# Moving two casts, four groups of transposes and one weight load by one step in a fused attention and SwiGLU kernel

## The chip, the cores and the metric

The kernel runs on one NeuronCore of one Trainium2 chip. The metric is the device time of one execution in microseconds; lower is better. The engines are named as the profile names them: PE is TensorE, PEld its weight loads, DVE is VectorE, ACT is ScalarE, POOL is GpSimd, SP is SyncE, which here only issues DMAs.

## The reference

Attention with a causal mask and a bias of cumulated sums, then a feed-forward block on the result (numpy, shortened):

```python
# q, k, v: (8, 8, 576, 64); s: (8, 8, 576); 4608 tokens, d_model 512, d_ff 1536
scores = scale * q @ k.T
cum = cumsum(maximum(s, 0))
scores = where(causal, -1e9, scores + minimum(-(cum[:, None] - cum[None, :]), 0))
attn = softmax(scores)
x = (attn @ v).transpose(0, 2, 1, 3).reshape(4608, 512)
out = (silu(x @ w_gate) * (x @ w_val)) @ w_out
```

Inputs and output are float32.

## The kernel before

All matrix products run in bfloat16. The work is one long list of instructions for each engine, written out in program order: each engine executes its own list from the top, and semaphores make it wait for the others. So the place of a call in the Python code sets the place of its instructions on every engine's list.

**Attention.** There are 64 heads, numbered 0 to 63 over batches (8 heads each). Four heads are a half batch (`hb`): half batch 2 is heads 8 to 11, half batch 3 is heads 12 to 15. For each half batch k and q are loaded as float32 (`load_one`, line 140, tiles `rawk` and `rawq`), cast to bfloat16 (`cast_one`, line 246 where GpSimd does it, tiles `ck` and `cq`), transposed and copied into the operand tile `kq`. For half batches 0 to 4 the transposition is done by TensorE: `pe_transpose` (line 287) makes five or four 128x128 transposes into a PSUM bank, and `pe_out` copies the two halves of the bank to `kq` (line 314 on ScalarE, line 316 on VectorE). `prep_one(hb, i)` is one such group: i = 0 and 2 are the two groups of k, 1 and 3 those of q. It issues the transposes and the first copy; the second copy goes on the list `seconds`, from which one is taken after every feed-forward item.

A head's scores are made in four pieces (`score_piece`, matmuls line 359, Exp on ScalarE line 369, tile `pt`). From head 8 on the causal mask is put on by a select on GpSimd after pieces 0 and 3 (lines 374 and 379). The attention-times-v products (`av_piece`, line 396) follow some heads later, and are normalised by VectorE (lines 412 and 413). v is cast in five chunks (`cast_v`, line 168, tile `vt`) as listed in `V1_AT`.

**Feed-forward.** 4608 tokens are taken in nine tiles of 512 (`tt`). Each tile has 12 gate blocks and 12 value blocks (`block`, line 629, four 128x512 matmuls each), a Tanh on ScalarE (line 650), two products on VectorE (lines 652 and 663), and then the down projection (line 686 for the first two tiles, line 735 for the others). Gate and value blocks are named here by their number: gate 5 is the sixth gate block of a tile.

**What sets the order.** The last loop of the kernel weaves the two together. `ffn_items(tt)` yields after every block or part of the down projection; its sum of costs is `n`. After each item the functions listed for this number by `at_item` are called, and then `pump` runs as many attention steps as belong to the share of the tile that is done. Inside `attn_items`, after piece `ci` of the head at place `step` of half batch `h`, the table `PREP_AT[h]` may call `prep_one` for the next half batch; for h = 2 ScalarE makes the copies if `ci` is 0 or 1, VectorE if it is 2 or 3. PSUM has eight banks; `take` gives the one that was released longest ago, in program order.

The stretch that the change touches lies in tile 0 of the feed-forward: heads 9 to 11 (half batch 2) are scored beside gate and value blocks 4 to 8, while k and q of half batch 3 are cast and transposed. Their loads were issued from GpSimd's list earlier. The output weights are loaded in two halves by `w_load("o", j)` (line 332), also issued by GpSimd. The v chunks of batch 1 and k and q of half batches 4 and 5 are issued by SP.

Of the kernel before, what the change touches and what calls it, by code (L numbers as in the profile page):

```python
# [19 lines left out]
def kernel(  # L20
# [11 lines left out]
    nc = tc.nc  # L32
# [77 lines left out]
    with tc.manual_schedule():  # L110
# [415 lines left out]
        def prep_one(hb, i, eng=None):  # L526
# [6 lines left out]
            seconds.append(lambda: pe_out(hb, nm, g, 1, eng))  # L533

        PREP_AT = {
            2: {(1, 2): 0, (2, 0): 2, (2, 2): 1, (3, 0): 3},
            3: {(1, 3): 0, (2, 1): 1, (2, 3): 2, (3, 1): 3},
        }

# [455 lines left out]
        def at_item(n, f, *args):  # L995
            hook[n].append(lambda: f(*args))

        at_item(2, prep_one, 2, 2)
        at_item(8, cast_one, 3, "k", nc.gpsimd)
        at_item(9, cast_one, 3, "q", nc.gpsimd)  # L1000
        at_item(10, w_load, "o", 0)
        at_item(12, w_load, "o", 1)
        for tt in range(NTT):
            lo = H * (tt + 1) + LAGS[tt]
# [60 lines left out]
```

## Time and profile before

| | us |
|---|---|
| median of 3 runs | 376.75 (376.2 to 377.3) |
| profiled execution: its own time | 375.79 |
| profiled execution: span of its instructions | 374.0 |
| TensorE busy | 360.7 |
| VectorE busy | 289.6 |
| ScalarE busy | 240.4 |
| GpSimd busy | 212.3 |
| DMA bandwidth, mean over the span | 172 GB/s |

The span is the time from the first to the last instruction; the device time of the same execution is 1.8 us longer. A matmul starts before the one in front of it has ended, so the busy time of TensorE holds no overlap twice, and distances are best counted from start to start. In a timeline, rows in a row with the same line are merged (x4), and a bracket gives the idle time of the engine before the row and what ended it. Some records of matmuls are missing, so that a block can be shown with three instead of four.

### The profile page before, as it was taken

Reading aid. Unit: us, or ns where it says so; the run is one execution under the profiler, and the core shown is the slowest. Engines: PE = TensorE matmul, PEld = TensorE weight load, DVE = VectorE, ACT = ScalarE, POOL = GpSimd, SP = SyncE. Lnnn points to the kernel's source line nnn. Section 1 sums busy time; section 2 is a strip of 40 time slices with the busy share of each in tenths; the row PEclk is TensorE's granted clock in tenths of the full one; section 3 lists DMA queues with packets and bytes.
Section 4 is the critical chain, followed back from the end, with each engine's and each line's share of the span. In section 5 each row is a group of like instructions: output and inputs, shape, how many; then the busy total and the mean of one; then the engine's idle time right before and its main releaser. Section 6 shows DMA issues by size and latency. Waiting matters only on the chain.

```text
span 374.0 us, 8759 instructions
## 1 busy us (share of the span) xinstructions
PE 360.7 (96%) x3259; PEld 230.6 (62%) x3300; DVE 289.6 (77%) x578; ACT 240.4 (64%) x471; POOL 212.3 (57%) x325
## 2 busy tenths in 40 slices
PE   7799899999999999999999999999999999999995
PEld 6584456655555556855685559655865585476464
DVE  8968776468995899588967997699858867975984
ACT  8777677698876877588757875686566523323321
POOL 8883555856455647494649464955675516315320
PEclk9999999999999999999999999999999999999999
DMA  7899999799877997896779675984132103002003
GB/s 239 193 258 253 219 257 267 237 303 247 245 186 220 254 262 196 178 281 205 211 167 266 178 182 174 255 206 98 40 119 62 35 19 128 2 0 95 20 0 114
DMA packets 97146, 64.23 MB, mean 172 GB/s; under 512 B 77232, under 2 KB 82736, under 8 KB 97104
## 3 DMA queue, kind: packets, MB, share of 16 engines
q1 hardware_dynamic: 84976, 41.46, 45.2%
q0 software_dynamic: 12128, 22.21, 22.6%
q8 instruction: 26, 0.43, 0.5%
q14 instruction: 16, 0.13, 0.1%
HBM read 37.90 MB, written 19.86 MB: 154 GB/s over the span
## 4 chain that ended last, share of the span: by engine, by line
PE 85%; DMA 6%; POOL 5%; ACT 1%; issue 1%; DVE 1%; DVEq 0%; POOLq 0%; ACTq 0%
PE bank L629 45%; PE bank L735 17%; PE bank L359 10%; PE bank L396 7%; PE bank L686 5%; DMA rawk<-in_k_dram 4%; DMA rawv<-in_v_dram 2%; POOL rawv L157 1%; POOL vt L168 1%; POOL wv L332 1%; ACT pt L369 1%; PE bank L287 0%; POOL rawq L140 0%; ACT kq L314 0%; POOL kq L211 0%
## 5 line engine op out<-in xcount | busy, mean ns | idle before, releaser
L369 ACT ACTIVATE pt<-bank 128x512 bf16<-128x512 f32 (+1 forms) x256 | 120.4, 510 | 31.0 <-PE bank L359 18.2
L629 PE MATMUL bank<-XT,wg 128*128 128x512 bf16 x418 | 110.3, 379 | 1.2 <-DVE pp L652 0.3
L629 PE MATMUL bank<-XT,wv 128*128 128x512 bf16 x412 | 109.3, 379 | 1.1
L650 ACT ACTIVATE th<-bank 128x512 bf16<-128x512 f32 x108 | 64.7, 599 | 55.9 <-PE bank L629 53.6
L652 DVE SCALAR_TENSOR_TENSOR pp<-th,bank 128x512 bf16<-128x512 bf16 x108 | 73.6, 682 | 19.2 <-ACT th L650 18.7
L663 DVE SCALAR_TENSOR_TENSOR ht<-pp,bank 128x512 bf16<-128x512 bf16 x108 | 74.1, 686 | 10.6 <-PE bank L629 0.4
L359 PE MATMUL bank<-kq 128*128 128x128 bf16 (+4 forms) x576 | 75.6, 240 | 1.5 <-DMA kq<-HL 1.0
L672 POOL TENSOR_TENSOR ht<-ht 128x512 bf16<-128x512 bf16 x35 | 40.4, 1154 | 52.2 <-DVE su L670 52.1
L359 PEld LDWEIGHTS <-kq 128*128 128x128 bf16 x576 | 45.8, 98 | 31.5 <-issue 1.9
L629 PEld LDWEIGHTS <-wv 128*128 128x128 bf16 x432 | 38.4, 98 | 36.5 <-issue 0.6
L629 PEld LDWEIGHTS <-wg 128*128 128x128 bf16 x432 | 38.3, 98 | 34.2 <-issue 0.7
L396 PEld LDWEIGHTS <-pt 128*128 128x128 bf16 x960 | 41.9, 98 | 17.2
L374 POOL TENSOR_SCALAR_AFFINE_SELECT pt<-pt 128x512 bf16<-128x512 bf16 x56 | 36.8, 658 | 27.3 <-ACT pt L369 22.7
L396 PE MATMUL bank<-vt,pt 128*128 128x65 bf16 x960 | 47.0, 194 | 0.4 <-POOL vt L168 0.3
L430 POOL DMA_DIRECT2D xs<-ot x24 | 21.7, 905 | 30.0 <-DVE ot L413 27.6
L735 PEld LDWEIGHTS <-ht 128*128 128x128 bf16 x336 | 31.2, 98 | 4.3
L413 DVE TENSOR_TENSOR ot<-bank,rc 128x320 bf16<-128x320 f32 x64 | 31.5, 492 | 2.2
L183 POOL DMA_DIRECT2D kq<-HL x48 | 28.9, 604 | 0.0
L735 PEld LDWEIGHTS <-su 128*128 128x128 bf16 x252 | 23.5, 98 | 3.3
L686 PE MATMUL bank<-wo,ht 128*128 128x512 bf16 x90 | 24.8, 379 | 0.3
L800 POOL TENSOR_TENSOR ysb<-ysb 128x512 f32<-128x512 f32 x12 | 15.2, 1270 | 15.3 <-DVE ysb L794 15.3
L379 POOL TENSOR_SCALAR_AFFINE_SELECT pt<-pt 128x64 bf16<-128x64 bf16 x56 | 14.8, 264 | 15.8 <-ACT pt L369 15.7
(93 smaller groups left out, 384.6 us busy)
## 6 DMA issues: line engine op xcount, KB each, us to landing
out_dram<-ysb POOLq DMA_DIRECT2D x32, 256.0 KB, 4.5
rawv<-in_v_dram SPq DMA_DIRECT2D x28, 256.0 KB
rawk<-in_k_dram SPq DMA_DIRECT2D x12, 576.0 KB
rawq<-in_q_dram SPq DMA_DIRECT2D x12, 576.0 KB
xs<-ot POOLq DMA_DIRECT2D x24, 160.0 KB, 3.5
ks<-ck SPq DMA_DIRECT2D x11, 288.0 KB
qs<-cq SPq DMA_DIRECT2D x11, 288.0 KB
rawk<-in_k_dram POOLq DMA_DIRECT2D x3, 576.0 KB, 7.3
```

The lines of the kernel that those rows point to most:

```text
L359: nc.tensor.matmul(sc[:, o : o + w], T[:, 1, e * S + 128 * tj : e * S + 128 * (tj + 1)], T[:, 0, e * S + lo : e * S + hi], start=not maske ...
L369: nc.scalar.activation(pt[:, c0 : c0 + n], sc, AF.Exp, scale=0.125)
L374: nc.gpsimd.affine_select(pt[:, 1088:1600], pt[:, 1088:1600], pattern=[[0, 4], [1, 128]], compare_op=ALU.is_ge, fill=zreg, base=0, channel ...
L396: nc.tensor.matmul(av[:, bi * (D + 1) : (bi + 1) * (D + 1)], pt[:, c0 : c0 + 128], VT[b % 2][:, tj, h, :], start=(tj == 0), stop=(tj == bi),)
L413: nc.vector.tensor_mul(ot[:, :, e * D : (e + 1) * D], av3[:, :, 0:D], rc[:, :, None].to_broadcast([128, NCH, D]),)
L629: nc.tensor.matmul(view(bs, TT), w[:, c, f0 : f0 + 128], xt[:, c, :], start=(c == 0), stop=(c == 3),)
L650: nc.scalar.activation(th, pg, AF.Tanh, scale=0.5)
L652: nc.vector.scalar_tensor_tensor(pp, in0=th, scalar=1.0, in1=pg, op0=ALU.add, op1=ALU.mult)
L663: nc.vector.scalar_tensor_tensor(hp[:, 2 * k2 : 2 * k2 + 2, :].rearrange("p a n -> p (a n)"), in0=pp, scalar=0.5, in1=pv, op0=ALU.mult, op ...
L672: (nc.vector if ft == NFT - 1 else nc.gpsimd).tensor_sub(hp[:, 1:3, :], hp[:, 1:4:2, :], hp[:, 0:3:2, :])
L686: nc.tensor.matmul(view(pys[ts_], DM), hps[ft // 2][:, 2 * (ft % 2) + half, c0 : c0 + 128], WO[j][:, ft % WKO, :], start=(ft == 0), stop=( ...
L735: nc.tensor.matmul(ps, lhs(p), rhs(p), start=(first and p == 0), stop=(last and p == NP - 1), skip_group_check=True,)
```

## The change

Three things move; no instruction is added or removed.

```diff
         PREP_AT = {
-            2: {(1, 2): 0, (2, 0): 2, (2, 2): 1, (3, 0): 3},
+            2: {(1, 3): 0, (2, 1): 2, (2, 3): 1, (3, 1): 3},
             3: {(1, 3): 0, (2, 1): 1, (2, 3): 2, (3, 1): 3},
         }
...
-        at_item(8, cast_one, 3, "k", nc.gpsimd)
-        at_item(9, cast_one, 3, "q", nc.gpsimd)
-        at_item(10, w_load, "o", 0)
+        at_item(9, cast_one, 3, "k", nc.gpsimd)
+        at_item(10, cast_one, 3, "q", nc.gpsimd)
+        at_item(9, w_load, "o", 0)
         at_item(12, w_load, "o", 1)
```

The four groups of transposes for half batch 3 come one score piece later: the first behind piece 3 of head 9 instead of piece 2, the second behind piece 1 of head 10 instead of piece 0, the third behind piece 3 of head 10 instead of piece 2, the last behind piece 1 of head 11 instead of piece 0. The engine of each copy stays the same. The two casts are listed after items 9 and 10 instead of 8 and 9, and the first half of the output weights after item 9, behind the cast of k, instead of after item 10.

## The prediction

> **What bounds the kernel now.** I read the page first: how full is TensorE, and where is it not full.
>
> ```profile
> span 374.0 us, 8759 instructions
> PE 360.7 (96%) x3259; PEld 230.6 (62%) x3300; DVE 289.6 (77%) x578; ACT 240.4 (64%) x471; POOL 212.3 (57%) x325
> ...
> PE   7799899999999999999999999999999999999995
> ...
> PEclk9999999999999999999999999999999999999999
> ```
>
> TensorE is busy 96% of the span at full granted clock, and all slices but the first two and the last are at 8 or 9 tenths. So a change outside TensorE counts only if it removes or adds TensorE idle time. The change works between 38 and 50 us; the waits of 22 to 60 us (total, times, longest) show what TensorE waits for there:
>
> ```profile
> PE bank L287 <- POOL ck L246: 1.2, 1, 1.2
> ...
> PE bank L396 <- POOL vt L168: 0.3, 1, 0.3
> ```
>
> The chain of waits of the same stretch (start, duration, what) says what stands behind these:
>
> ```profile
> 22.81 15.78 DMA rawk<-in_k_dram
> ...
> 38.72 1.15 POOL ck L246
> ...
> 39.92 0.45 PE bank L287 x5
> ...
> 47.45 0.69 DVE pp L652
> ...
> 48.17 0.84 DVE kq L316
> ...
> 49.03 0.70 DVE ht L663
> ...
> 50.55 0.24 POOL pt L379
> ...
> 53.66 0.19 PE bank L396
> ```
>
> Three places follow: the load of k for half batch 3 lands, GpSimd casts it, and the first transposes (39.92) start the moment the cast is done; VectorE's product for value block 7 (49.03) frees the bank of gate block 9 (49.77); a select on GpSimd (50.55) lets the casts of v start, and TensorE waits for the fourth (53.66). Last the timelines of TensorE, of GpSimd and of ScalarE:
>
> ```profile
> 38.38 0.38 PE L359 MATMUL bank<-kq 128*128 128x320 bf16 x2
> 39.92 0.45 PE L287 MATMUL bank<-ident,ck 128*128 128x128 bf16 x5 [1.16 <-POOL ck L246]
> 40.21 0.19 PE L359 MATMUL bank<-kq 128*128 128x64 bf16 x1
> 40.24 1.03 PE L629 MATMUL bank<-XT,wg 128*128 128x512 bf16 x4
> 41.10 0.39 PE L359 MATMUL bank<-kq 128*128 128x128 bf16 x4
> ```
>
> ```profile
> 38.72 1.14 POOL L246 CAST ck<-rawk 128x1152 bf16<-128x1152 f32 x1 [1.51 <-DMA rawk<-in_k_dram]
> ...
> 40.21 1.15 POOL L246 CAST cq<-rawq 128x1152 bf16<-128x1152 f32 x1 [0.35 <-DMA rawq<-in_q_dram]
> 41.30 0.85 POOL L332 DMA_DIRECT2D wo<-in_moe_w_out_dram  x1
> ```
>
> ```profile
> 47.29 0.72 ACT L314 COPY kq<-bank 64x512 bf16<-64x512 bf16 x1
> ...
> 49.02 0.72 ACT L314 COPY kq<-bank 64x512 bf16<-64x512 bf16 x1
> 49.77 1.20 ACT L369 ACTIVATE pt<-bank 128x512 bf16<-128x512 f32 x3
> ```
>
> Matmuls overlap, so I count from start to start. A 128x512 costs 0.216 us, a block of four 0.86 to 0.87 (40.24 to 41.10), a piece 3 of a head 0.03, a piece 2 0.22. The first transposes were due at 38.38 + 0.22 = 38.60 and began at 39.92: **1.32 us lost**. Gate 9 was due at 49.47 (piece 0 of head 12 at 49.25 plus 0.22) and began at 49.77: **0.30 lost**. The tenth product of head 8's first attention-times-v piece was due at 53.22 and began at 53.66: **0.44 lost**. After it TensorE's largest idle time is 0.12 us, at 85.49; small gaps of 0.05 are rows where a matmul record is missing.
>
> **The change, part by part.** It adds and removes no instruction. Comparing the built orders:
>
> *Casts.* On GpSimd only the cast of q and the first output-weight issue change places; the cast of k stays where it was. So its time stays too: it waits for a landing that TensorE does not influence, and ends at 39.86.
>
> *First transposes.* Between piece 2 of head 9 and these transposes TensorE now has piece 3 (0.03) and gate 5 (0.86). They are due at 38.60 + 0.89 = 39.49 and still start at 39.92: 0.43 lost instead of 1.32, **0.89 saved**. Both items that move forward wait for banks released by 37 us.
>
> *The rest of the stretch, to gate 9.* The other three transpose groups and their eight copies to kq also move one piece later. On ScalarE the Tanh of gate 6 started at 43.31 and that of gate 7 at 46.81; between them stand two kq copies, two 512-wide Exps, then a 64-wide and a 512-wide Exp. The changed order has the same six there. VectorE then has product, kq copy, product (47.45, 48.17, 49.03 to 49.73) in both orders. Gate 6 ends 0.89 earlier, so the chain does, and gate 9 starts at 48.88; TensorE's own due time moves as much (48.58), so the 0.30 stays lost. Nothing gained or lost here.
>
> *A new tight place.* The last transposes now follow head 11's piece 1 and gate 8: 46.83 - 0.89 + 0.21 + 0.87 = 47.02, done at 47.41. Their first copy on ScalarE comes behind gate 8's Tanh (47.2 to 47.7), so about 47.70 to 48.40. Head 12's piece 0, the first reader, is due at 48.36: 0.1 late where it was 1.2 early. That 0.1 hides in the wait before gate 9; gate 8, value 8 and the pieces of head 11 are the cover. If the copy is over 0.3 late, every further tenth is lost.
>
> *v casts.* The second copy of the last q group (49.02) stood in front of head 11's pieces 2 and 3 on ScalarE; now it stands behind them. Piece 2 starts at 48.44 after the first copy. Its row at 49.77 was followed by the select at 50.55 (+0.78) and the fourth v cast's end at 53.60 (+3.05). The same steps give 49.22 and 52.27. TensorE wants it at 53.22 - 0.89 = 52.33: the 0.44 goes, **0.4 saved**. If ScalarE is as late as before relative to TensorE, none of it goes. The v loads that these casts read had landed by 50.97 by their semaphore events; the cast of the last one comes at about 52.2.
>
> *Output weights.* Issue (0.85) from 39.86 instead of 41.30; the cast of q then runs 40.71 to 41.86, 0.5 later. Its reader, the third transposes, stands at 43.7: 1.9 us of cover. Queued behind on GpSimd are the selects of heads 9 and 10 and the second weight issue, none read before 50 us. At no cover this would cost 0.5. The weights are read from 57 us on; the first landed at 51.69.
>
> *DMA.* 1.4 us earlier the weight load can take packets from SP's queue, which carries v (batch 1) and k, q of half batch 4. The landed load of k was at hand when its cast started at 54.30 without a wait; its transposes, at 57.58 before, would be due at 56.25. With the cast's 1.14 the load may land until 55.1. Even if all 1.4 us were taken from it, from the 53.87 of its semaphore events, the delay costs 0.2. I take nothing: the software queue was still full with older weights until 45.47 (wv's landing). By the Trainium skill ("DMA: Bandwidth & Descriptors", section "Queues, rings and completion order") each DMA engine takes turns between queues packet by packet, which speaks against issuing weights early: by it SP's loads would give up about half of 1.4 us, an estimate of 0.7, and the sum would still not change, as 53.87 + 0.7 is within the limit.
>
> *To the end.* From head 12's first attention-times-v piece on, the orders of all engines agree but for bank names, so whatever TensorE is ahead at 53 us, it stays ahead, unless a transfer is late. Nearest: half batch 6's transposed k landed at 93.32, and the copy reading it on VectorE began at 93.77. Ahead by 1.3, that copy waits up to 0.9. At 127.35 the same copy waited 0.34 and TensorE lost nothing.
>
> **Sum.** 0.89 + 0.44 = 1.33. On the profiled execution's own time, 375.79 (span 374.0, 1.8 around it, unchanged): 374.46. That execution lies 0.96 under the median, 376.75; on the median 375.4. Bounds: 0.89 alone gives 375.9; with the tight place 0.3 worse, 376.2; with the 0.30 before gate 9 gone too, 375.1.
>
> **Rivals.** *The wait returns at head 12 or downstream.* The first 0.89 is real, but the copies of q are now the last thing ready, or later loads land at fixed times and eat the lead. For: 0.1 late by my own walk, and 1.3 us less room; the 0.45 at 93 us. Against: the copies have only ScalarE's order to fear, and VectorE's wait at 127 us did not reach TensorE. Price: 0.5 to 1.3 given back, 375.9 to 376.75.
>
> *Slower: the early weights push back SP's loads.* Place: the load of k 4, or the last of v, which GpSimd casts in order ahead of everything else. It decides from a landing of k 4 later than 55.1; to end 1.13 over the median it must take back 1.33 + 1.13, so land at 57.6, 3.7 us later than now. For: DMA is saturated there (page: 9 tenths). Against: the issue moves by 1.4 us, no bytes are added. Time 377.9.
>
> *It does nothing:* the cast of k does not move on GpSimd, so were the transposes' wait set by a later landing than the profile's, by 0.4 or more, the saving remains 0.89. Only an earlier landing takes it away: by 0.9 it leaves 0.4 of the 0.89, by 1.3 nothing: 376.3 to 376.75.
>
> **Chances.** Forecast 0.74; given back 0.10; nothing 0.05; slower 0.11. About 0.3%, 1.13 us, is what a measurement of this kernel can tell from no change, so faster begins under 375.6. The forecast's own range, 374.9 to 375.9, lies mostly below that: I put 0.66 of its 0.74 there, and 0.08 inside. Faster 0.66; within 0.08 + 0.10 + 0.05 = 0.23; slower 0.11. Range: 374.5 (the bound 375.1 less 0.6, as the lowest run of before lies 0.55 under its median) to 376.7, which takes in nearly all of the give-back.
>
> **What would show it.** After: transposes of k at 39.9 with an idle of about 0.3 instead of 1.16; gate 5 at 38.63; gate 9 at 48.9; the wait of the attention-times-v product on v under 0.1; the cast of q at 40.7. Wrong: a TensorE wait on the kq copy before head 12's piece 0 over 0.3; gate 9 later than 49.2; a wait of the k 4 transposes at 56; a span above 373.3.

## The result, and the profile after

The changed kernel is slower: 378.95 us (median of 14 runs, 377.27 to 380.65) against 376.16 us (14 runs, 374.42 to 378.36) of the kernel before. The ratio is 1.0074, with a 95% interval of 1.0053 to 1.0096. The forecast was 375.4 us with a range from 374.5 to 376.7. The profiled execution of the changed kernel took 377.27 us, the lowest of its 14. The top of its page:

```profile
span 375.6 us, 8799 instructions
...
PE 363.3 (97%) x3300; PEld 231.1 (62%) x3300; DVE 290.1 (77%) x578; ACT 240.8 (64%) x471; POOL 213.1 (57%) x325
...
PE   7799979999999999999999999999999999999995
...
PEclk9999999999999999999999999999999999999999
```

The averages say almost nothing. (More matmuls are listed than before because fewer records are missing, not because there are more.) The waits from 22 to 62 us (total, times, longest) say where the time went:

```profile
PE bank L396 <- POOL vt L168: 2.5, 1, 2.5
...
POOL vt L168 <- DMA rawv<-in_v_dram: 2.4, 1, 2.4
```

The wait of the transposes (L287) is gone; about 0.3 of it was forecast to stay. But the attention-times-v product's wait on the cast of v, which was to go from 0.44 (counted from start to start; 0.28 by its bracket) to under 0.1, grew to 2.5. The cast itself now waits 2.4 for its load. The chain of waits (start, duration, what) shows the load:

```profile
33.45 21.05 DMA rawv<-in_v_dram
54.51 0.05 issue
54.56 0.63 POOL vt L168
55.19 0.04 issue
55.23 0.19 PE bank L396
55.42 0.86 PE bank L629 x4
```

In the kernel before, what ended this chain at the same place was a select on GpSimd, and the load did not appear. Now chunk 3 of v (batch 1) lands at 54.5; by its semaphore events it landed at 46.75 before. The timeline of GpSimd around it:

```profile
49.75 1.17 POOL L168 CAST vt<-rawv 128x512 bf16<-128x512 f32 x2
50.93 0.64 POOL L374 TENSOR_SCALAR_AFFINE_SELECT pt<-pt 128x512 bf16<-128x512 bf16 x1
51.51 0.61 POOL L168 CAST vt<-rawv 128x512 bf16<-128x512 f32 x1
54.56 1.28 POOL L168 CAST vt<-rawv 128x512 bf16<-128x512 f32 x2 [2.43 <-DMA rawv<-in_v_dram]
```

Chunks 0 to 2 are cast in time, then GpSimd stands still until chunk 3 is there. TensorE at the places that the prediction had put times on, with gate 7 (44.66) between them:

```profile
39.02 0.41 PE L359 MATMUL bank<-kq 128*128 128x320 bf16 x3
39.27 1.03 PE L629 MATMUL bank<-XT,wg 128*128 128x512 bf16 x4
40.13 0.44 PE L287 MATMUL bank<-ident,ck 128*128 128x128 bf16 x5
...
44.19 0.39 PE L359 MATMUL bank<-kq 128*128 128x128 bf16 x4
44.66 1.02 PE L629 MATMUL bank<-XT,wg 128*128 128x512 bf16 x4
...
47.94 1.03 PE L629 MATMUL bank<-XT,wv 128*128 128x512 bf16 x4
48.97 0.38 PE L359 MATMUL bank<-kq 128*128 128x128 bf16 x4
49.19 1.03 PE L629 MATMUL bank<-XT,wg 128*128 128x512 bf16 x4
...
52.25 0.44 PE L396 MATMUL bank<-vt,pt 128*128 128x65 bf16 x9
55.23 0.19 PE L396 MATMUL bank<-vt,pt 128*128 128x65 bf16 x1 [2.54 <-POOL vt L168]
```

To compare these with the trace of before, one offset must be taken off: the first feed-forward matmul (L629) began at 25.80 before and at 26.44 here. That is 0.64 later and lies in front of everything that the change touches. Counted from there, gate 5 stands at 38.63 and gate 9 at 48.55, and the first transposes (40.13) have no idle time at all. Up to 52 us TensorE was ahead as forecast, and somewhat more. Then nine products of head 8 run and the tenth waits 2.54 us.

Why would chunk 3 come late, if no byte was added? The DMA queues in two stretches of 3 us (packets, MB, share of 16 engines): q1 is SP's queue with v, k and q, q0 the software queue, which GpSimd fills, with the weights. The share adds up the times of all packets, which overlap, so it can pass 100%. First the kernel before, 41 to 44 us (upper two lines) and 44 to 47 us (lower two):

```profile
q0 software_dynamic: 442, 0.33, 70.1%
q1 hardware_dynamic: 1202, 0.30, 56.2%
...
q0 software_dynamic: 441, 0.44, 89.6%
q1 hardware_dynamic: 895, 0.22, 34.5%
```

The same stretches of the changed kernel:

```profile
q1 hardware_dynamic: 1785, 0.45, 72.5%
q0 software_dynamic: 320, 0.26, 54.0%
...
q0 software_dynamic: 560, 0.57, 113.1%
q1 hardware_dynamic: 168, 0.04, 10.8%
```

A chunk of v is 1024 packets of 256 bytes. Between the older weights and the output weights the software queue runs empty, engine by engine, and SP's queue then goes fast. By the DMA packets of the trace, in before it carries about 190 packets per us up to 42 us, 347 in the next, then 664 and 723 in the two us from 43 to 45, while q0 falls from about 190 to 158, 93 and 74. I call this the hole. Chunks 2 and 3 go through in it. In the changed kernel the hole is over at 44, and for three us, beside output weights in packets of about 1 KB, SP's queue carries 54 to 58 packets per us. In the changed kernel the output weights were issued at 38.89 (41.30 before) and ended the hole early: of chunk 3, ten of the 16 DMA engines were through by 44.2, and the other six finished at 46.9, 50.0, 51.4, 51.7, 52.1 and 54.5. Over 41 to 47 us SP's queue carried only 144 packets fewer (1953 against 2097), but the load is complete only with its last packet.

### The profile page after: what moved, and what is told of

Read it like the earlier page. It is cut to its first block, busy times and chain, and to the rows that moved or that the text cites. A ratio compares the mean times of both kernels' runs of the same rounds, so it can differ in the third digit from the quotient of the medians.

```text
span 375.6 us, 8799 instructions
## 1 busy us (share of the span) xinstructions
PE 363.3 (97%) x3300; PEld 231.1 (62%) x3300; DVE 290.1 (77%) x578; ACT 240.8 (64%) x471; POOL 213.1 (57%) x325
## 4 chain that ended last, share of the span: by engine, by line
PE 86%; DMA 7%; SPq 2%; POOL 2%; ACT 1%; issue 0%; DVEq 0%; POOLq 0%; DVE 0%
PE bank L629 45%; PE bank L735 17%; PE bank L359 11%; PE bank L396 7%; DMA rawv<-in_v_dram 6%; PE bank L686 6%; SPq L157 2%; ACT pt L369 1%; DMA kq<-HL 1%; PE bank L353 1%; PE bank L287 0%; PE bank L445 0%; POOL kq L214 0%; POOL kq L211 0%; POOL rawk L140 0%
## 5 line engine op out<-in xcount | busy, mean ns | idle before, releaser
L629 PE MATMUL bank<-XT,wg 128*128 128x512 bf16 x432 | 111.4, 379 | 0.4 <-DVE pp L652 0.3
L629 PE MATMUL bank<-XT,wv 128*128 128x512 bf16 x432 | 110.9, 379 | 0.1
L672 POOL TENSOR_TENSOR ht<-ht 128x512 bf16<-128x512 bf16 x35 | 40.5, 1156 | 52.1 <-DVE su L670 52.0
L629 PEld LDWEIGHTS <-wv 128*128 128x128 bf16 x432 | 38.4, 98 | 38.7 <-issue 2.9
L629 PEld LDWEIGHTS <-wg 128*128 128x128 bf16 x432 | 38.4, 98 | 34.2 <-issue 0.7
L686 PE MATMUL bank<-wo,ht 128*128 128x512 bf16 x96 | 25.7, 379 | 0.0
```

Of the source, the lines that this page charges most:

```text
L629: nc.tensor.matmul(view(bs, TT), w[:, c, f0 : f0 + 128], xt[:, c, :], start=(c == 0), stop=(c == 3),)
L672: (nc.vector if ft == NFT - 1 else nc.gpsimd).tensor_sub(hp[:, 1:3, :], hp[:, 1:4:2, :], hp[:, 0:3:2, :])
L686: nc.tensor.matmul(view(pys[ts_], DM), hps[ft // 2][:, 2 * (ft % 2) + half, c0 : c0 + 128], WO[j][:, ft % WKO, :], start=(ft == 0), stop=( ...
```

## The experiments

Theory: the early output weights alone cause the loss, by catching the last packets of chunk 3; the moved transposes are a gain of about 1.3 that this hides. Rivals: the transposes' new place costs something that the walk missed; the weights cost by their bytes and not by where they overtake; the clock after the wait is the larger part. All ratios are to the kernel before on the same chip.

**The weights alone, and the transposes alone.** Two kernels split the change. The first is the kernel before with only the first output weights issued early:

```diff
         at_item(8, cast_one, 3, "k", nc.gpsimd)
+        at_item(8, w_load, "o", 0)
         at_item(9, cast_one, 3, "q", nc.gpsimd)
-        at_item(10, w_load, "o", 0)
```

> The kernel before with one part of the change alone: the first half of the output weights is issued on GpSimd between the casts of k and q of half batch 3; casts and transposes stay. Theory A (the early weights reach the DMA engines before SP's load of v chunk 3 is through them; chunk 3 lands at 54.5 us instead of 46.8, its cast and TensorE wait for it): chunk 3 lands after 50 us, TensorE waits 1 to 2.5 us before the tenth attention-times-v product of head 8, and because that wait ends at a landing, not at TensorE's own pace, the time is the changed kernel's, 378 to 379.5, 0.4% to 0.9% over before. Theory B (the later transposes and kq copies, or the new order of banks, cost the time): no difference from before, within 0.3%, and the first transposes still wait for the cast.

Measured: 379.15 us (6 runs), ratio 1.0079 [1.0053, 1.0105], as slow as the whole change. Its waits from 22 to 62 us:

```profile
PE bank L396 <- POOL vt L168: 3.1, 1, 3.1
...
POOL vt L168 <- DMA rawv<-in_v_dram: 2.7, 1, 2.7
```

Chunk 3 landed at 55.5, with nine of its engines through by 45.2. The first transposes, at their place in the kernel before, waited only 0.08 us here, because k had landed at 38.34 and TensorE came to them 0.8 later. That this is as slow as the whole change is itself a reading: the gain from the transposes cannot show in a kernel where TensorE later waits for a landing, since being early only makes that wait longer.

The second is the changed kernel with the weights issued behind the cast of q again:

```diff
         at_item(10, cast_one, 3, "q", nc.gpsimd)
-        at_item(9, w_load, "o", 0)
+        at_item(11, w_load, "o", 0)
```

> The changed kernel with the weight issue put back behind the cast of q (one 64-wide select later than in the kernel before). Theory A: v chunk 3 lands before 48 us, the wait before the tenth product is under 0.1 us, and the predicted 0.9 to 1.3 us are gained: 374.8 to 375.5, 0.2% to 0.4% under before. Theory B: as slow as the changed kernel, about 379.

Measured: 374.87 us (12 runs), ratio 0.9974 [0.9951, 0.9998]. By the ratio that is 0.98 us less than before, with an interval of 0.1 to 1.8 that holds the predicted 1.33. Its timeline of GpSimd:

```profile
49.79 1.17 POOL L168 CAST vt<-rawv 128x512 bf16<-128x512 f32 x2
50.97 0.63 POOL L374 TENSOR_SCALAR_AFFINE_SELECT pt<-pt 128x512 bf16<-128x512 bf16 x1
51.55 1.72 POOL L168 CAST vt<-rawv 128x512 bf16<-128x512 f32 x3
```

The casts of chunks 2 to 4 follow one another with no bracket: chunk 3 had landed at 47.8. The weights, issued at 41.39, landed at 51.99, as in the kernel before (41.30 and 51.69). This version is faster than both kernels, against the kernel before by an interval that ends just under 1.

**Later still.** The first weights at item 12, the second half at item 15.

```diff
-        at_item(9, w_load, "o", 0)
-        at_item(12, w_load, "o", 1)
+        at_item(12, w_load, "o", 0)
+        at_item(15, w_load, "o", 1)
```

> The changed kernel with both halves of the output weights issued later: the first behind the select of head 10's piece 0 (about 43 us, where the second stood), the second two selects later (about 47 us). Theory A: the software queue stays empty longer after the older weights, v chunk 3 lands by 46 us or earlier and chunk 4 by 50; time as with the weights behind the cast of q or up to 0.3 us better, 374.5 to 375.4, unless the second half, read from about 66 us, comes too late. Theory B: about 379.

Measured: 375.01 us (12 runs), ratio 0.9979 [0.9952, 1.0006]. Chunk 3 landed at 46.2. In its profile the first weights were issued at 41.41, hardly later than in e2 (41.39), not at about 43 as expected; the second half came at 46.00 instead of 42.83. So a later second half won nothing that these runs can tell apart, and a much later first half was not tried. Three of its 12 runs took 377.7 to 380.2 at a mean granted clock of 0.991 to 0.995; what slowed those was not looked into.

**The change again**, with no edit, on another occasion:

> The changed kernel once more, in the same job as the three others, for a second profile. Theory A: v chunk 3 lands after 50 us again, though not at the same time, and the wait before the tenth product is 2 us or more; time 0.5% to 1.0% over before. If the wait is far longer than 2.5 us in this profile, the granted clock should be lower after it, as the recorded runs with clocks of 0.994 and spans of 377.3 against 0.999 and 375.6 suggest.

Measured: 379.91 us (6 runs), ratio 1.0112 [1.0085, 1.0138]; chunk 3 at 55.1. The waits, and then two windows (length, busy time of TensorE, weight load, VectorE, ScalarE, GpSimd, then granted clock, DMA share, GB/s):

```profile
PE bank L396 <- POOL vt L168: 3.4, 1, 3.4
POOL vt L168 <- DMA rawv<-in_v_dram: 3.2, 1, 3.2
```

```profile
54.00:58.00 4.00, 2.20 (x14) 1.09 (x14) 0.24 (x1) 0.00 (x0) 2.14 (x4) 0.61 1.00 361
58.00:62.00 4.00, 4.00 (x28) 2.25 (x27) 1.96 (x6) 1.54 (x3) 2.21 (x3) 0.53 0.77 207
```

Here is a second cost that the first profile did not have: from 54.91 on, the last 0.9 us of the wait and what follows, TensorE's granted clock is 0.5 for 6.8 us, and in 58 to 62 us it gets 28 matmuls done where the first profile of the changed kernel had 57. By the Trainium skill ("TensorE: Matmul & The Clock Gate", section "Part 1: The HAM clock gate (the "warmup" mystery)") the clock falls to half after an idle window of about 3.4 us, and the windows run free of the kernel. The stretches seen here, 3.4 and 6.8 us, are one and two such windows. But the clock also fell after waits of 3.07 and 3.26 us, shorter than the page's window, and did not after 2.54. Where they differ, the runs decide.

The records of the granted clock in the traces show what decides here besides the length: how the wait lies against the windows. All but the last of each trace, which the end cuts off, last whole multiples of 3.41 us, so the windows of each trace can be counted. In the first profile of the changed kernel a new window began at 53.88, in the middle of the wait: 1.19 us of idle time fell into one window and 1.35 into the next, and the clock stayed. In e1, e4, e5 and e7 a single window held 2.78, 2.48, 1.95 and 2.49 us of idle time, and the clock fell at that window's end (55.90, 54.91, 57.04 and 56.18). In e4 it stayed at half for one more window, which held the last 0.89. This is read from five traces; the place of a wait was not varied by itself.

**Bytes or overtaking?** The early weights stay, but chunks 3 and 4 of v go into the same queue, issued by GpSimd ahead of them:

```diff
-        load_v(1, range(5))
+        load_v(1, range(3))
+        load_v(1, (3, 4), nc.gpsimd)
```

> The changed kernel, early weights and late transposes, with chunks 3 and 4 of v (batch 1) issued from GpSimd at about 30 us, in the same software queue ahead of the output weights, instead of from SP. Theory A (the weights overtake these chunks because they come through the other queue): both chunks land before 48 us, no wait before the tenth product, first weights land about 1.5 us later than in the changed kernel; time as with the weights behind the cast of q, 374.5 to 375.5. A rival within A (what counts is the bytes that the early weights add before 50 us, whatever the queue): something else lands late instead, chunk 2 or k of half batch 4, and the time stays above 377.

Measured: 374.63 us (12 runs), ratio 0.9981 [0.9956, 1.0007]. The weights were issued at 39.16, about as early as in the changed kernel, and the same bytes were moved. GpSimd again:

```profile
50.03 1.17 POOL L168 CAST vt<-rawv 128x512 bf16<-128x512 f32 x2
51.21 0.63 POOL L374 TENSOR_SCALAR_AFFINE_SELECT pt<-pt 128x512 bf16<-128x512 bf16 x1
51.79 1.72 POOL L168 CAST vt<-rawv 128x512 bf16<-128x512 f32 x3
```

No wait. Chunks 3 and 4 landed at 46.4 and 47.0. So an early issue by itself costs nothing that these runs can tell apart, nor do its bytes: it costs when it overtakes, from another queue, a load that is needed sooner. The two chunks changed their time of issue with their queue (30.7 and 31.6 instead of 33.5 and 39.2), and the two were not tried apart.

**Earlier still.** The first weights at item 7, issued at 34.65:

```diff
-        at_item(9, w_load, "o", 0)
+        at_item(7, w_load, "o", 0)
```

> The changed kernel with the first output weights issued still earlier, at about 35.5 us, in front of the selects of heads 8 and 9 and of the cast of k. Theory A: the software queue does not run empty at all between the older weights and these, so SP's queue never gets its stretch of 340 to 720 packets per us; chunk 3 and now chunk 2 too land later than in the changed kernel on more engines, chunk 3 at 54 to 57; wait of 3 us or more, half clock after it, 380 to 383. If what counts were only the swap with the cast of q: as the changed kernel, 379.

Measured: 379.47 us (4 runs), ratio 1.0092 [1.0059, 1.0126]. The queues, 41 to 44 us (upper two) and 44 to 47 us (lower two):

```profile
q0 software_dynamic: 525, 0.44, 90.4%
q1 hardware_dynamic: 530, 0.13, 33.7%
...
q0 software_dynamic: 471, 0.47, 92.4%
q1 hardware_dynamic: 464, 0.12, 29.7%
```

The hole is gone: 994 packets of SP's queue in 6 us where before had 2097. Chunk 3 now lands late on all 16 engines (52.2 to 54.5) instead of on six. In the end that costs the same, because only the last engine counts; TensorE waited 3.26.

**Half the size.** Three of the six slices of the first output weights are issued early, the other three at item 15, and the second load (`"o", 1`) at item 16:

```diff
+            if kind == "o" and h is not None:
+                dst, src_ap = dst[:, 3 * h : 3 * h + 3], src_ap[:, 3 * h : 3 * h + 3]
...
-        at_item(9, w_load, "o", 0)
-        at_item(12, w_load, "o", 1)
+        at_item(9, w_load, "o", 0, 0)
+        at_item(15, w_load, "o", 0, 1)
+        at_item(16, w_load, "o", 1)
```

> The changed kernel with only half of the early load (three of six slices of the first output weights) issued at the early place; the other half and the second weights are issued at about 47 us. Theory A: the engines that the early half catches before v chunk 3 is through are free again about 3 us sooner; chunk 3 lands at 48 to 51, its cast comes at its place in GpSimd's order or up to 0.5 us after; time 374.5 to 376. If the early start alone decided, whatever the size: chunk 3 at 54 or later and 379.

Measured: 374.65 us (10 runs), ratio 0.9976 [0.9954, 0.9998]. Issued at 38.66, chunk 3 at 48.2, no wait. It moves the rest of the weights too, so it does not isolate size from what follows: from 47 to 50 us the software queue carried nothing. Together with the late chunk of e7 it fits SP's packets being slowed for as long as any weights, of either half, are queued beside them.

**The clock.** Is the rest of the loss the half clock? Spare 128x128 matmuls on a bank of their own fill the wait for chunk 3, first 36, then 66. They stand in front of the seventh product:

```diff
+                        if p == H:
+                            fill = take()
+                            for _ in range(36):
+                                nc.tensor.matmul(view(fill, 128), ident, ident, start=True, stop=True)
+                            give(fill)
```

> The changed kernel with 36 matmuls of 128x128 on a spare bank (identity by identity, result unused, 36 x 0.056 = 2.0 us) put on TensorE in front of the product that waits for v chunk 3. The wait itself is not shortened. If the idle time alone is the cost (theory A without the clock): 379 to 380, no better than the changed kernel. If, as the two profiles with waits of 3.07 and 3.37 us and a clock of 0.5 for 3.4 and 6.8 us after them suggest, a part of the cost is the granted clock (theory A with the clock): the clock stays at full after the wait, the idle rest is 0.5 to 1.5 us, and 1.5 to 3 us come back: 376 to 377.5. Theory B (transposes or bank order): 379 or more.

Measured: 379.33 us (6 runs), ratio 1.0092 [1.0061, 1.0123]. In its profile 1.95 us of wait were left, chunk 3 came at 55.1, and the clock still fell, to 0.5 for 3.4 us, from 57.04 on, 1.2 us after the wait had ended. In the five other runs the mean clock was 1.0, and yet they took 378.2 to 380.5.

> The changed kernel with 66 instead of 36 spare matmuls in front of the product that waits for v chunk 3 (66 x 0.056 = 3.7 us), so that TensorE is busy through nearly the whole wait, which still ends with the landing at 54.5 to 55.5 us. If the granted clock is a part of the cost: idle rest under 0.5 us, no stretch at 0.5 near 55 us, and about 1.7 us (half of 3.4 us) come back against the changed kernel: 377 to 377.8. If the clock is no part of it, or falls for another reason: 379 to 380, as with 36 spare matmuls, where the idle rest was 1.95 us and the clock fell all the same.

Measured: 378.73 us (9 runs), ratio 1.0095 [1.0063, 1.0128]. The windows of this kernel:

```profile
54.00:58.00 4.00, 3.95 (x71) 3.52 (x70) 0.49 (x2) 0.00 (x0) 1.42 (x3) 1.00 1.04 363
58.00:62.00 4.00, 3.95 (x48) 2.57 (x46) 3.38 (x8) 2.91 (x6) 3.33 (x5) 1.00 0.85 234
```

The clock stays at 1.00 through both. But the time did not come back. In this profile the fill itself ran until 56.59, some 0.8 beyond the end of the cast, which uses up half of what the clock would give. Counted from the first feed-forward matmul, the tenth product came at 30.20 (e5) and 29.77 (e9), later than in the first profile of the changed kernel (28.79), whatever the clock did. So the larger fill keeps the clock up, but these two runs do not show by their times what the half clock costs. That is left to the traces, below.

**The kernel before once more**, with no edit, for a second trace:

> The kernel before, for a second profile of it. The wait of the first transposes for the cast of k was 1.16 us in the first profile, and 0.08 us in the kernel with the early weights alone, whose TensorE order is the same: there TensorE reached the place 0.8 us later and the load landed 0.3 us earlier. If the wait depends on this, it lies anywhere between 0 and 1.2 us here and follows from the landing of k (36.9 to 38.6 in the profiles so far) less TensorE's own arrival; chunk 3 of v lands before 48 us. If it is fixed by the order, it is 1.0 to 1.2 again.

Measured: 376.36 us (one run, span 374.6). Its waits:

```profile
PE bank L287 <- POOL ck L246: 1.2, 1, 1.2
...
PE bank L396 <- POOL vt L168: 0.3, 1, 0.3
```

The load of k landed at 39.16, chunk 3 at 47.2. Both waits that the prediction worked with were there again, 1.24 and 0.28. They are no accident of one execution, though the first was 0.08 in e1.

## Why the prediction was wrong

**Steps that held.** *First transposes* and *the rest of the stretch*: less the offset of 0.64, gate 5 stands at 38.63, the forecast place, and gate 9 at 48.55 (forecast 48.9). In its parts the walk was less exact, and that the errors nearly cancel is luck. The transposes had no idle time at all, where 0.3 was forecast, because the load of k landed 10.4 us after the first feed-forward matmul in that execution (at 36.86), not 12.8 (38.60). In all nine traces with late transposes it was 10.4 to 12.4, and at most 0.08 was lost. That also explains the cast of q at 39.73 instead of 40.7. Gate 7, due at 44.41, began at 44.66: 0.25 was lost where nothing was forecast. *A new tight place*: head 12's piece 0 began 0.05 after the copy's end (48.92 to 48.97). It was due at 48.81, so 0.16 was lost, near the forecast 0.1. Gate 9 then follows at 49.19 with nothing lost: the 0.30 before it, which was to stay, went. *Output weights*, as a matter of GpSimd's order: the later cast of q held up nobody.

**The sum of the saved terms came out near, where it could show.** From the first feed-forward matmul to the tenth product of head 8 it took 27.86 us before and 27.93 in its second trace, and 26.30, 26.31, 26.28 and 26.31 in the four kernels with the late transposes and no late chunk (e2, e3, e6, e8). That is 1.6 us; 1.33 was forecast. Up to gate 9 it is 1.2 (forecast 0.89), and from there to the tenth product 0.35 (forecast 0.44): about 0.2 of the wait on v stayed, now for the cast and not for a load. How much of the 1.6 is owed to the move depends on when k lands: e1, which has the old order but got k at 11.7, reached gate 9 in 22.88 us, against 22.76 in e2 and 23.97 before. So the trace gain is mostly there when k lands as late as in the two traces of before (12.8 and 12.9). The timed gain of e2 is 0.98, with its wide interval. The late sign that was named, a wait of the transposes of half batch 4, showed in e2 at 57.06, with 0.20 us idle and 0.37 from start to start; the prediction had allowed for 0.2.

**To the end** held in part. From the tenth product to the end of the span it took 320.33 and 320.34 in the two traces of before, and 320.33 in the changed kernel. But the changed kernel is behind there, not ahead. Of the four that are ahead, e6 and e8 kept their lead (319.96 and 320.30), while e2 took 320.69 and e3 320.90: e2 gave back its 0.37 at 57.06, and e3 most of its 0.57 at 117.92, where TensorE waited for the load `XT<-xs`. So the rival of a lead given back downstream came true in part in two kernels of four.

**The step that failed is *DMA*,** the one that reads "I take nothing: the software queue was still full with older weights until 45.47". Two things in it were wrong. First, 45.47 is the landing of the older weights, the time of their last packet on the last engine. The queue was not full until then. It ran empty engine by engine from 42 us on, and early output weights filled the places as they came free. Second, the delay was bounded by the shift of the issue ("even if all 1.4 us were taken"), but a caught load is not late by as much as the other was early. Chunk 3 landed 7.75 us later (46.75 to 54.5) for an issue that was 2.4 us earlier in that trace. A chunk has 64 packets on each of the 16 engines (1024 in all). In the hole the last engine took 0.94 us for them: chunk 2 landed at 45.81, chunk 3 at 46.75. Beside the weights it took 6.58: 47.93 and 54.51. The slowing outlasts the load that was moved, which had landed at 49.27; behind it stood the second half of the output weights, which landed at 55.61. Before gave rows for such a bound: the two halves, issued at 41.30 and 43.04, landed at 51.69 and 60.15. Chunk 3, landing at 46.75, was wanted by GpSimd at about 51.7 (its cast of 0.6 was to end at 52.27). It had 5 us to spare, and that is no cover while weights are queued beside it for longer.

The rival "the early weights push back SP's loads" had the right mechanism and a chance of only 0.11. It named the wrong load, k of half batch 4 or the last of v; the one that mattered was chunk 3, a load that was through on ten engines when the early weights filled the queue. And it set the point of decision at a delay of 3.7 us, which it took to be out of reach. The page on DMA that the prediction weighed ("DMA: Bandwidth & Descriptors", section "Queues, rings and completion order") spoke against the change in the right direction. The estimate of 0.7 us drawn from it was a tenth of what came, because it halved the shift instead of counting packets. Turns by packet agree with the traces where both queues had work throughout: about 190 packets per us each beside the older weights, and in e7, from 45 to 51 us, 150 to 162 of SP's against 151 to 159 of the output weights. At that rate 1024 packets take about 6.6 us, an estimate, and chunk 3's last engine took 6.58. The 54 to 58 per us in the changed kernel from 44 to 47 are no other rule: six engines of 16 at the rate of e7 would carry about 58, also an estimate, and six were still at chunk 3. Why the other ten carried none of SP's packets meanwhile is not shown.

**A cost that no step had** is the clock. From the tenth product to the end of the span, by trace:

| trace | tenth product waits, us | clock after it | to the end of the span, us |
|---|---|---|---|
| before; again | 0.28; 0.28 | full | 320.33; 320.34 |
| changed | 2.54 | full | 320.33 |
| e9, filled | none | full | 320.33 |
| e1 | 3.07 | 0.5 for 3.4 us | 321.79 |
| e7 | 3.26 | 0.5 for 3.4 us | 321.96 |
| e5, partly filled | 1.95 | 0.5 for 3.4 us | 321.97 |
| changed again (e4) | 3.37 | 0.5 for 6.8 us | 323.39 |

So 3.4 us of half clock cost 1.5 to 1.6 us, and 6.8 us cost 3.1. Of the 14 runs of the changed kernel, ten had a mean granted clock of 0.991 to 0.995 and a median of 379.3; the four at 0.998 or more had a median of 377.7.

**The account of the +2.79 us in the median**: the tenth product comes 0.9 us (changed) to 1.7 us (e4) later, counted from the first feed-forward matmul (28.79 and 29.61 against 27.9); in most runs 1.5 to 3.1 us of half clock follow. The low ends, 0.9 + 1.5 = 2.4, lie a little under the difference of the medians. How much of it is the clock was not settled by timing: the two filled kernels kept the clock up in most runs and were no faster.

## What to carry to other kernels

When a load is issued earlier, list every load that is still on the way in other queues at the new time, with its reader's due time. The cover that it needs is measured by how long the other queue's loads last, those queued behind the moved one included, not by the shift. A landing time is the last packet of the slowest DMA engine, so it does not say that the queue was full until then. And a part that gains can be hidden wholly by a part that makes a landing late, so the two are to be tried apart: with the weights left where they were (e2) the late transposes won about 1 us, by an interval of 0.1 to 1.8.

## What the runs showed of the hardware that was not expected

- A load can be caught on some DMA engines only: chunk 3 was through on ten of 16 by 44.2 us and on the last at 54.5.
- SP's queue with 256-byte packets went at 664 to 723 packets per us while the software queue ran empty, and at 150 to 162 beside weights in packets of about 1 KB, which went at 151 to 159 (e7, 45 to 51 us): as many packets of each, though the one is four times the other.
- TensorE's granted clock fell to 0.5 after waits of 1.95 us (with about 2 us of small spare matmuls in front), 3.07, 3.26 and 3.37 us, and did not after 2.54. In the four that fell, 1.95 to 2.78 us of the idle time lay within one window of 3.41 us; the 2.54 was split into 1.19 and 1.35. Where between 1.35 and 1.95 the limit lies, and how it depends on what TensorE does otherwise, is open.
